# Attention in blocks of 32 keys, head pairs by quadrant, probabilities turned in place on VectorE

## The chip, the core and the metric

The kernel runs on one core of a Trainium2 chip. Its engines are named as in the profile: PE (TensorE, the 128x128 array for matrix products), PEld (its weight loads), DVE (VectorE), ACT (ScalarE), POOL (GpSimd) and SP (SyncE, which issues the transfers). The metric is the time of one execution in device microseconds; lower is better.

## What is computed

```python
# q, k, v: 8 batches x 8 heads x 576 x 64; x: 4608 x 512; w_in 512 x 1024, w_out 1024 x 512 (float64)
q_d, k_d, v_d = (means over 4 neighbours along the sequence)          # 144 rows each
out_up = repeat(softmax(scale * q_d @ k_d.T) @ v_d, 4)                # pooled attention
mask = abs(i - j) < 4
out_local = softmax(where(mask, scale * q @ k.T, -1e9)) @ v           # local attention
x = (out_up + out_local), heads side by side                          # 4608 x 512
h = x @ w_in
solu = h * softmax(h)
ln = (solu - mean) / sqrt(var + 1e-6) * g_ln
out = ln @ w_out                                                      # 4608 x 512
```

## The kernel before

The output rows fall into 36 FFN tiles of 128 rows. Each needs its rows of x, which attention makes batch by batch, 576 rows at a time, transposed: x lies with 128 partitions for the two heads of a pair and four pairs side by side.

**Local attention** of a batch is five units of two windows each, 64 keys for 58 queries. In a unit PE makes the scores (tile sc, L606 or L694: 16 fp32 matmuls, each on a 64x64 quarter of the array, which appear as 32 records in the trace), DVE adds the mask and takes the maximum, POOL or DVE subtracts it, ACT takes the exponential, DVE the sum and its reciprocal, POOL or DVE multiplies. The probabilities (pl) have to be turned. In batches 0 to 2 and in each batch's last unit PE does it (plt, L654, four transposes) and ACT or DVE copies the result out of PSUM (plT, L262 or L264). In batches 3 to 7 units go in pairs: eight transfers move 32-wide pieces (plT<-pl), and DVE transposes 128x1024 in 32x32 squares (L745). Then PE multiplies with the values (xp, L664 or L752), and the result is stored or added to x (L577).

**Pooled attention** goes by head pair, four times a batch: sd (L787, six matmuls of 144 keys), maximum (L794), three exponentials (L802), reciprocal and multiplication (L809, L811), 12 transposes on PE (pdt, L822), two copies (pdT), the product with the pooled values (po, L843), accumulation with each column written four times (L577).

**The FFN** splits x into a high and a low part in fp32r (xh, xl) and the weights likewise, and forms each product from three: h (L861, 24 matmuls of 128x512 for each half of 512 columns and both halves) and o (L985, 24). Between them stand the softmax chain (nmx, e, su, nmu), a trip through DRAM that turns u (u<-e, v<-u, then the DVE transposes of L962), and the split into uh and ul (L968, L971). The last tile's u is turned on PE (ut).

q and k of batches 0 and 1 are turned on PE (qp, kp, L556), later ones by DVE (L462, L466). The kernel also issues 24 pairs of filler matmuls (warm, L1042) in its first stages. PSUM: ps_a two buffers of two banks for everything of attention, ps_t one bank (plt, po), ps_h two banks (h), ps_o one bank (o).

All steps stand in a list, and the numbers in ORDER set the order in which they are issued; this is the order on every engine. A number that is also in OTHER swaps the engine of that step for its alternative (`engine(usual, instead)`). Nothing reorders at run time: an engine that waits holds up what stands behind it.

Of the kernel before, what the change touches and what calls it, by code (L numbers as in the profile page):

```python
# [136 lines left out]
def pooled_local_attention_then_solu_ffn(  # L137
# [33 lines left out]


# [980 lines left out]
```

## Time and profile before

| | us |
|---|---|
| median of 3 runs (lowest, highest) | 593.27 (591.71, 594.09) |
| span of the profiled execution | 592.8 |
| idle time of PE in the span | 24.3 |
| ACT busy, POOL busy | 335.9, 317.8 |
| moved by DMA | 99.58 MB in 207112 packets |

The page gives no time of the profiled execution other than its span, which is 0.5 us below the median. Busy times are sums over an engine's instructions. A PE matmul's start is recorded and its end modelled, so distances are taken from start to start. In a row of the trace, "sc<-kT,qT 64*64 64x64 f32 x32" means 32 records that make sc from kT and qT, with a tile of 64x64 of the array and 64 moving columns; the tiles that follow a "<-" with an engine in brackets are what the engine waited for. One fp32 matmul gives two records (two passes) and two weight loads.

### The profile page before, as it was taken

The page shows a single profiled execution, that of the slowest core. Times are in us where ns is not written, and L with a number is a line of the kernel's source. Part 1 is how long each engine was busy: PE and PEld are TensorE (multiplying, and loading weights), DVE is VectorE, ACT ScalarE, POOL GpSimd, SP SyncE. Part 2 cuts the span into 40 slices and gives each one's busy share as a digit, 9 for nine tenths or more (in the row PEclk, how much of TensorE's full clock was granted, in tenths as well). Part 3 has the DMA queues.
Part 4 walks back from the last instruction along what each step waited for, and adds up shares of the span by engine and source line. Part 5 has one row for each costly group of instructions (what it writes and reads, how often), then busy time and mean ns, then how long its engine had stood idle before and what let it go on. Part 6 is the DMA issues. An engine that isn't in the chain of part 4 may idle for free.

```text
span 592.8 us, 15179 instructions
## 1 busy us (share of the span) xinstructions
PE 568.5 (96%) x5832; PEld 439.3 (74%) x5832; DVE 468.1 (79%) x769; ACT 335.9 (57%) x751; POOL 317.8 (54%) x465
## 2 busy tenths in 40 slices
PE   8789799999989999999999999999999999999996
PEld 5567567677767777777777777787787777778885
DVE  6987999999898989887988968978885854654441
ACT  3577677785555655574457455575445645434443
POOL 2475799577765735485366734354532676242211
PEclk9698999999999999999999999999999999999999
DMA  9998779777787688785897858765535454332331
GB/s 272 237 239 168 162 178 201 184 143 210 178 190 179 147 235 183 173 209 169 194 187 186 203 155 156 214 150 177 159 101 159 133 143 139 106 126 90 124 108 53
DMA packets 207112, 99.58 MB, mean 168 GB/s; under 512 B 163136, under 2 KB 193344, under 8 KB 207040
## 3 DMA queue, kind: packets, MB, share of 16 engines
q1 hardware_dynamic: 207040, 98.61, 66.5%
q8 instruction: 46, 0.75, 0.6%
q14 instruction: 26, 0.21, 0.1%
HBM read 65.54 MB, written 27.79 MB: 157 GB/s over the span
## 4 chain that ended last, share of the span: by engine, by line
PE 72%; DVE 10%; SPq 4%; DMA 4%; issue 4%; POOL 3%; ACT 2%; DVEq 0%; POOLq 0%; ACTq 0%
PE h L861 28%; PE o L985 27%; SPq L285 3%; PE sd L787 2%; PE po L843 2%; PE xp L752 2%; PE pdt L822 2%; PE kp L556 2%; PE warm L1042 2%; PE qp L556 1%; PE sc L694 1%; DMA qm<-in_q_dram 1%; DMA u<-e 1%; POOL xl L1019 1%; PE sc L606 1%
## 5 line engine op out<-in xcount | busy, mean ns | idle before, releaser
L861 PE MATMUL h<-wi_h,xh 128*128 128x512 f32 x288 | 116.6, 405 | 0.9 <-DVE e L876 0.7
L985 PE MATMUL o<-wo_h,uh 128*128 128x512 f32 x288 | 116.4, 404 | 0.8 <-ACT uh L968 0.7
L861 PE MATMUL h<-wi_h,xl 128*128 128x512 f32 x288 | 114.3, 397 | 2.6 <-DVE xl L1019 1.4
L985 PE MATMUL o<-wo_l,uh 128*128 128x512 f32 x288 | 113.9, 395 | 0.0
L861 PE MATMUL h<-wi_l,xh 128*128 128x512 f32 x288 | 113.8, 395 | 0.0
L985 PE MATMUL o<-wo_h,ul 128*128 128x512 f32 x288 | 79.0, 395 | 0.0
L869 DVE TENSOR_REDUCE nmx<-h 128x1 f32<-128x1024 f32 x36 | 43.5, 1209 | 36.0 <-PE h L861 36.0
L873 ACT ACTIVATE e<-h,nmx 128x1024 f32<-128x1024 f32 x36 | 40.1, 1113 | 49.8 <-DVE nmx L869 46.0
L861 PEld LDWEIGHTS h<-wi_h,xl 128*128 128x128 f32 x288 | 54.1, 188 | 16.8 <-POOL xl L1019 2.0
L861 PEld LDWEIGHTS h<-wi_h,xh 128*128 128x128 f32 x288 | 54.1, 188 | 16.0 <-DVE e L876 1.9
L985 PEld LDWEIGHTS o<-wo_h,uh 128*128 128x128 f32 x288 | 54.0, 188 | 15.8 <-issue 1.6
L985 PEld LDWEIGHTS o<-wo_h,ul 128*128 128x128 f32 x288 | 54.0, 188 | 13.3 <-DVE ul L971 0.3
L861 PEld LDWEIGHTS h<-wi_l,xh 128*128 128x128 f32 x288 | 54.1, 188 | 12.0
L985 PEld LDWEIGHTS o<-wo_l,uh 128*128 128x128 f32 x288 | 54.1, 188 | 11.9
L971 POOL TENSOR_TENSOR ul<-v,uh 128x512 fp32r<-128x512 f32 x37 | 48.3, 1312 | 24.7 <-ACT uh L968 20.9
L876 DVE SCALAR_TENSOR_TENSOR e<-h,e 128x1024 f32<-128x1024 f32 x36 | 43.7, 1213 | 16.7 <-ACT e L873 16.5
L968 ACT ACTIVATE uh<-v 128x512 fp32r<-128x512 f32 x70 | 42.5, 623 | 21.0 <-DVE v L962 16.9
L962 DVE STREAM_TRANSPOSE v<-v 128x512 f32<-128x512 f32 x70 | 46.6, 688 | 4.8 <-DMA v<-u 4.8
L992 ACT ACTIVATE osb<-o,s 128x512 f32<-128x512 f32 x36 | 24.6, 682 | 43.3 <-PE o L985 18.3
L1019 POOL TENSOR_TENSOR xl<-x,xh 128x512 fp32r<-128x512 f32 (+1 forms) x31 | 37.6, 1219 | 16.5 <-ACT xh L1016 16.0
L881 POOL TENSOR_SCALAR nmu<-su 128x1 f32<-128x1 f32 x36 | 9.8, 273 | 67.0 <-DVE e L876 56.7
L899 ACT ACTIVATE e<-e,nmu 128x1024 f32<-128x1024 f32 x29 | 33.3, 1148 | 19.7 <-POOL nmu L881 19.7
(122 smaller groups left out, 1142.6 us busy)
## 6 DMA issues: line engine op xcount, KB each, us to landing
u<-e SPq DMA_DIRECT2D x35, 512.0 KB
v<-u SPq DMA_DIRECT2D x140, 128.0 KB
vs<-in_v_dram SPq DMA_DIRECT2D x32, 288.0 KB
out_dram<-osb SPq DMA_DIRECT2D x36, 256.0 KB
qm<-in_q_dram SPq DMA_DIRECT2D x96, 72.0 KB
km<-in_k_dram SPq DMA_DIRECT2D x96, 72.0 KB
vw<-in_v_dram SPq DMA_DIRECT2D x80, 64.0 KB
vw<-in_v_dram SPq DMA_DIRECT2D x40, 128.0 KB
```

The source lines that it names most:

```text
L285: nc.sync.dma_start(t[nm][Q * 32:Q * 32 + 32, pr], src[b, 2 * pr + par, :, dh * 32:dh * 32 + 32].rearrange("(k t) d -> t k d", t=32),)
L861: nc.tensor.matmul(hps[:, n, :], src[:, cc, :], wt[:, cc, n * 512:(n + 1) * 512], start=(cc == 0 and src is xh and wt is wi_h), stop=(cc = ...
L869: nc.vector.tensor_reduce(out=nmx, in_=hf, op=ALU.max, axis=AX.X, negate=True)
L873: nc.scalar.activation(e, hf, AF.Exp, bias=nmx, scale=1.0, accum_out=se)
L876: nc.vector.scalar_tensor_tensor(out=e, in0=hf, scalar=1.0, in1=e, op0=ALU.mult, op1=ALU.mult, accum_out=su)
L899: nc.scalar.activation(e, e, AF.Identity, bias=nmu, scale=1.0)
L962: nc.vector.transpose(vg, vg)
L968: nc.scalar.activation(uh, tp, AF.Copy)
L971: (usual if v is None else engine(usual, nc.vector)).tensor_tensor(out=ul, in0=tp, in1=uh.bitcast(F32), op=ALU.subtract)
L985: nc.tensor.matmul(o, src[:, j, :], wt[:, 4 * g + j, :], start=(g == 0 and j == 0 and src is uh and wt is wo_h), stop=(g == 1 and j == 3 a ...
L992: nc.scalar.activation(osb, o, AF.Copy, scale=s)
L1019: engine(nc.gpsimd, nc.vector).tensor_tensor(out=l, in0=src, in1=h.bitcast(F32), op=ALU.subtract)
```

## The change

- Windows of local attention have 32 keys for 24 queries. A unit holds eight windows (w selects one of four quadrants of 32 partitions, g one of two windows there), a batch three units. sc is 64 matmuls on 64x32 tiles of the array with 32 moving columns, twice as many tiles as before; xp comes in two halves of 32 matmuls on 32x64 tiles with 24 moving columns.
- Pooled attention goes by blocks of 29 queries, with the four head pairs in the four quadrants; five blocks in two slots, three and two. sd is 24 or 16 matmuls on 64x32 tiles; po two halves of 20 matmuls on 32x64 tiles with 87 or 58 moving columns.
- All keys of a window lie within one 32x32 square, so DVE turns the probabilities in place (in pl and pd), for every batch. The transposes on PE (plt, pdt), their copies, and the plT transfers are gone, and pl and pd are fixed buffers of three each.
- ps_t is gone; ps_o has two buffers; po uses ps_a.
- The values of a unit are loaded in four steps with two transfers each (64 KB, 32 rows x 8 heads x 64).
- ORDER and OTHER are new (places below). Paths that were switched off (MASKED, SUMS_ON_PE, G_LATE, FIRST_ON_PE) are removed. The FFN's code is the same.

The core of the diff:

```diff
-    W = 64
-    starts = [0] + [58 * w - 3 for w in range(1, 9)] + [S - W]
-    qlo = [58 * w for w in range(9)] + [520]
-    qhi = qlo[1:] + [S]
+    KB = 32
+    QW = 24
+    GW = 2
+    NU = S // (4 * GW * QW)
+
+    def window(u, w, g):
+        n = 4 * GW * u + GW * w + g
+        s0 = min(max(QW * n - (KB - QW) // 2 + 1, 0), S - KB)
+        return s0, QW * n - s0
+
+    QS = 29
+    SLOTS = ((0, 3), (3, 5))
+    QPAD = QS * 4 + KB
+    NKB = -(-SD // KB)
+    PDW = NKB * KB
...
-    ps_t = ctx.enter_context(tc.tile_pool(name="ps_t", bufs=1, space=PSUM))
     ps_h = ctx.enter_context(tc.tile_pool(name="ps_h", bufs=1, space=PSUM))
-    ps_o = ctx.enter_context(tc.tile_pool(name="ps_o", bufs=1, space=PSUM))
+    ps_o = ctx.enter_context(tc.tile_pool(name="ps_o", bufs=2, space=PSUM))
...
-    pls = [cpool.tile([P, NPR * LP], F32, name=f"pl_{n}") for n in range(4)]
+    NG = 2 * GW * NPR
+    pls = [cpool.tile([P, NG, KB + 1], F32, name=f"pl_{n}") for n in range(3)]
+    pds = [cpool.tile([P, 2, 3, PDW], F32, name=f"pd_{n}") for n in range(3)]
...
+    def load_vw(vw, b, u, w):
+        for g in range(GW):
+            s0, _ = window(u, w, g)
+            nc.sync.dma_start(
+                vw[w * KB:(w + 1) * KB, g], v[b, :, s0:s0 + KB, :].rearrange("h s d -> s h d")
+            )
...
+            sc = two_banks(*scores_bank(b, u), f"sc_{b}_{u}")[:, :, 0:GW * NPR * KB]
+            at = sc.rearrange("p a (g r k) -> p a g r k", g=GW, r=NPR)
+            for g in range(GW):
+                for pr in range(NPR):
+                    for n in range(8):
+                        w, par = n // 2, (n + n // 2) % 2
+                        s0, _ = window(u, w, g)
+                        nc.tensor.matmul(
+                            at[w * KB:(w + 1) * KB, par, g, pr],
+                            bt.qT[rows(par), pr, s0:s0 + KB], bt.kT[rows(par), pr, s0:s0 + KB],
+                            start=True, stop=True,
+                        )
+            yield
+            pl_all = pls[(NU * b + u) % len(pls)]
+            pl = pl_all[:, :, 0:KB]
+            mx = small.tile([P, NG], F32, tag="mxl", name=f"mxl_{b}_{u}")
...
+            engine(nc.gpsimd, nc.vector).tensor_tensor(
+                out=pl, in0=pl, in1=sm.unsqueeze(2).broadcast_to([P, NG, KB]), op=ALU.mult
+            )
+            yield
+            nc.vector.transpose(pl, pl)
+            yield
+            plT = pl.rearrange("p (a g r) k -> p a g r k", a=2, g=GW)
+            for half in range(2):
+                xp = two_banks(ps_a, "a", f"xp_{b}_{u}_{half}")[:, :, 0:NPR * GW * QW]
+                at = xp.rearrange("p a (r g n) -> p a r g n", r=NPR, g=GW)
+                for g in range(GW):
+                    for pr in range(NPR):
+                        for n in range(4):
+                            a, par = n // 2, (n + n // 2) % 2
+                            w = 2 * half + a
+                            _, a0 = window(u, w, g)
+                            ks = slice(w * KB, (w + 1) * KB)
+                            nc.tensor.matmul(
+                                at[rows(par), a, pr, g],
+                                bt.vw[u][ks, g, 2 * pr + par, :],
+                                plT[ks, par, g, pr, a0:a0 + QW], start=True, stop=True,
+                            )
                 yield
+                t0 = QW * GW * (4 * u + 2 * half)
+                accumulate(
+                    bt.out()[:, :, t0:t0 + 2 * GW * QW].rearrange("p r (a n) -> p r a n", a=2),
+                    xp.rearrange("p a (r n) -> p r a n", r=NPR), self.first,
...
+            sd = two_banks(*scores_bank(b, n), f"sd_{b}_{n}")[:, :, 0:ns * SD]
+            sd = sd.rearrange("p a (s k) -> p a s k", s=ns)
+            for s in range(ns):
+                for i in range(8):
+                    w, par = i // 2, (i + i // 2) % 2
+                    nc.tensor.matmul(
+                        sd[w * KB:(w + 1) * KB, par, s],
+                        qd_all[rows(par), w, QS * (s0 + s):QS * (s0 + s) + KB],
+                        bt.kd[rows(par), w, :], start=True, stop=True,
+                    )
...
+            pd_all = pds[(2 * b + n) % len(pds)][:, :, 0:ns]
+            pd = pd_all[:, :, :, 0:SD]
...
+            engine(nc.gpsimd, nc.vector).tensor_tensor(
+                out=pd, in0=pd, in1=sm.unsqueeze(3).broadcast_to([P, 2, ns, SD]), op=ALU.mult
+            )
+            yield
+            nc.vector.transpose(pd_all, pd_all)
+            yield
+            pdT = pd_all.rearrange("p a s (k q) -> p a s k q", k=NKB)
+            for half in range(2):
+                po = two_banks(ps_a, "a", f"po_{b}_{n}_{half}")[:, :, 0:ns * QS]
+                for kb in range(NKB):
+                    nk = min(KB, SD - kb * KB)
+                    for i in range(4):
+                        a, par = i // 2, (i + i // 2) % 2
+                        w = 2 * half + a
+                        ks = slice(w * KB, w * KB + nk)
+                        nc.tensor.matmul(
+                            po[rows(par), a].rearrange("p (s q) -> p s q", s=ns),
+                            bt.vd[ks, par, kb, :], pdT[ks, par, :, kb, 0:QS],
+                            start=kb == 0, stop=kb == NKB - 1,
+                        )
                 yield
+                q0 = QS * s0
+                xv = bt.out()[:, 2 * half:2 * half + 2, FAC * q0:FAC * (q0 + nq)]
+                accumulate(
+                    xv.rearrange("p r (s f) -> p r s f", f=FAC),
+                    po[:, :, 0:nq].unsqueeze(3).broadcast_to([P, 2, nq, FAC]), self.first,
                 )
                 yield
...
         late = bt.b == 0
+        local = [Local(bt, u, not late) for u in range(NU)]
+        pooled = [Pooled(bt, n, late) for n in range(2)]
+        values(bt)
         for it in pooled + local if late else local + pooled:
+            if isinstance(it, Local):
+                for w in range(4):
+                    step(bt.load_v, it.u, w)
+                row(it.steps(), 12)
+            else:
+                row(it.steps(), 10)
 
```

PE's order at one place in mid-run, before. Names are tile_batch_unit (sc, xp), tile_batch_pair (po) or tile_number (h, o); the last number of each is a running one. These rows stand between h_10 and the first half of o_7:

```order
L694 MATMUL sc_4_0_3346<-kT_4_2932,qT_4_3037 64x2x32 x16
L694 MATMUL sc_4_1_3364<-kT_4_2932,qT_4_3037 64x2x32 x16
L843 MATMUL po_3_1_3382<-pdT_3_1_3146,vd_3_3074 64x144 x4
L752 MATMUL xp_3_0_3387<-plT_3_0_3182,vw_3_0_2969 64x64 x16
L752 MATMUL xp_3_2_3404<-plT_3_2_2980,vw_3_2_3034 64x64 x16
L985 MATMUL o_7_3448<-wo_h_117,uh_7_0_3330 128x512
```

PE's order of the changed kernel ahead of the same o_7, which now comes behind h_9 (po_2_1_0 is batch 2, slot 1, half 0):

```order
L670 MATMUL h_9_3404<-wi_h_132,xl_9_3360 128x512
L531 MATMUL sc_3_2_3443<-kT_3_2800,qT_3_3053 32x32 x64
L531 MATMUL sc_3_0_3514<-kT_3_2800,qT_3_3053 32x32 x64
L531 MATMUL sc_3_1_3587<-kT_3_2800,qT_3_3053 32x32 x64
L647 MATMUL po_2_1_0_3684<-pd_2_122,vd_2_2194 64x58 x20
L794 MATMUL o_7_3731<-wo_h_134,uh_7_0_3509 128x512
```

The three sc of batch 3 have moved together; po stands behind them, and xp has moved elsewhere.

DVE's order, batch 3 in mid-run, before, at the turning of its pairs of units (mxd and rsd belong to pooled attention, v_7 to the FFN, qT_4 and kT_4 to the next batch):

```order
L264 COPY pdT_3_0_3165<-pdt_3_0_3152 72x6x48
L466 STREAM_TRANSPOSE qT_4_3037<-qm_4_2467 128x576
L264 COPY plT_3_4_3273<-plt_3_4_3167 128x512
L962 STREAM_TRANSPOSE v_7_3124<-v_7_3124 128x4x128 x2
L794 TENSOR_REDUCE mxd_3_2_3294<-sd_3_2_3246 128x3
L745 STREAM_TRANSPOSE plT_3_0_3182<-plT_3_0_3182 128x1024
L809 RECIPROCAL rsd_3_3_3323<-smd_3_3_3078 128x3
L745 STREAM_TRANSPOSE plT_3_2_2980<-plT_3_2_2980 128x1024
```

DVE's order of the changed kernel, from the sum of unit 0 of batch 3 to its turn:

```order
L555 TENSOR_REDUCE sml_3_0_3714<-pl_0_114 128x16
L556 RECIPROCAL sml_3_0_3714<-sml_3_0_3714 128x16
L780 TENSOR_TENSOR ul_7_1_3667<-v_7_3374,uh_7_1_3666 128x512
L771 STREAM_TRANSPOSE v_8_3657<-v_8_3657 128x4x128
L368 TENSOR_REDUCE qd_all_130<-qT_3_3053 128x144
L562 STREAM_TRANSPOSE pl_0_114<-pl_0_114 128x16x32
L414 STREAM_TRANSPOSE kT_4_3755<-km_4_3721 128x576
L233 COPY x_3_3842<-xp_3_0_0_3809 128x4x96
```

The turn (L562) has moved from a place long behind its unit's reciprocal to four rows behind it, and the copies of pdT and plT are gone; the values' product xp is stored two rows further on.

Of ORDER, 2039 numbers before and 1827 now, one line each:

```diff
-23 16 165 166 2 4 167 168 169 170 171 24 26 27 25 28 29 3 172 33 32 30 31 173 174 197 17 175
+1 32 22 9 24 147 148 26 27 34 35 149 131 25 28 150 33 151 152 132 133 134 29 153 135 136 137 30
```

More of the change, by code (lines that the diff above doesn't have):

```diff
@@ L271, in scores_bank @@
         return (ps_h, "h") if b < 1 and n % 2 else (ps_a, "a")
-    def small_bank(b, n):
-        return (ps_o, "o") if b < 2 and n % 2 and not WARM else (ps_t, "t")
     def load_q_k(t, b, pr):
@@ L434, in __getattr__ @@
             elif what == "qd":
-                self.qd = [
-                    qd_flat[:, (NPR - 1 - pr) * SD:(NPR - pr) * SD] for pr in range(NPR)
-                ]
+                self.qd = [qd_all[:, pr, 0:SD] for pr in range(NPR)]
             elif what == "kd":
@@ L475, in out, with pooled_vload, pooled_vsum @@
             return xs[self.b]
-        def value(self, kc, head):
-            return [self.vd[:, kc, head, :]]
-        def pooled_vload(self, c, hs):
-            self.vs[c, hs.start] = load_vs(self.b, c, hs)
-        def pooled_vsum(self, c, hs):
-            vs = self.vs.pop((c, hs.start))
+        def pooled_vload(self, n):
+            if n == 2:
+                self.vs[n] = tails[self.b % len(tails)]
+                load_tail(self.vs[n], self.b)
+                return
+            t = big(f"vs_{self.b}_{n}").rearrange("p (k x) -> p k x", k=NKB - 1)
+            load_vs(t, self.b, n)
+            self.vs[n] = t
+        def pooled_vsum(self, n):
+            vs = self.vs.pop(n)
+            out = self.vd[:, :, NKB - 1] if n == 2 else self.vd[:, n, 0:NKB - 1]
             eng = engine(nc.gpsimd, nc.vector)
@@ L489, in pooled_vsum @@
             eng.tensor_tensor(
[L490 removed]
+                out=out, in0=vs[:, :, 0:D], in1=vs[:, :, D:2 * D], op=ALU.add
             )
[L493 to L516 removed]
     class EarlyBatch(Batch):
@@ L593, in steps @@
             b = bt.b
-            early = b < MASKED
-            sc = two_banks(*scores_bank(b, u), f"sc_{b}_{u}")
-            if early:
-                for a in range(2):
-                    nc.tensor.matmul(
-                        sc[:, a, 0:NPR * W].rearrange("p (r w) -> p r w", w=W), ident_b,
-                        mask_b.unsqueeze(1).broadcast_to([P, NPR, W]), start=True, stop=False,
-                    )
-            for pr in range(NPR):
-                for par, wi in TILES:
-                    s0 = starts[2 * u + wi]
-                    nc.tensor.matmul(
-                        sc[rows(wi), par ^ wi, pr * W:(pr + 1) * W],
-                        bt.qT[rows(par), pr, s0:s0 + W], bt.kT[rows(par), pr, s0:s0 + W],
-                        start=not early, stop=not early or pr == NPR - 1,
-                    )
@@ L635, in steps @@
-            nc.scalar.activation(by_pair, by_pair, AF.Exp, scale=SCALE)
-            yield
-            sm = small.tile([P, NPR, 2], F32, tag="sml", name=f"sml_{b}_{u}")
-            nc.vector.tensor_reduce(
-                out=sm, in_=pl_all.rearrange("p (r a w) -> p r a w", r=NPR, a=2), op=ALU.add, axis=AX.X
-            )
-            rs = small.tile([P, NPR, 2], F32, tag="rsl", name=f"rsl_{b}_{u}")
-            nc.vector.reciprocal(out=rs, in_=sm)
+            sc = two_banks(*scores_bank(b, u), f"sc_{b}_{u}")[:, :, 0:GW * NPR * KB]
@@ L643, in steps @@
             yield
             engine(nc.gpsimd, nc.vector).tensor_tensor(
-                out=pl, in0=pl, in1=rs.unsqueeze(3).broadcast_to([P, NPR, 2, W]), op=ALU.mult
-            )
-            yield
-            q0, q1 = qlo[2 * u], qhi[2 * u + 1]
-            nw = (q1 - q0) // 2
-            a0 = [qlo[w] - starts[w] for w in (2 * u, 2 * u + 1)]
-            pool, tag = small_bank(b, u)
-            pt = pool.tile([P, NPR, 2, W], F32, tag=tag, name=f"plt_{b}_{u}")
-            for pr in range(NPR):
-                nc.tensor.transpose(pt[:, pr, :, :], by_pair[:, pr], ident)
@@ L655, in steps @@
-            yield
-            plT = wk.tile([P, NPR, 2, W], F32, tag="plT", name=f"plT_{b}_{u}")
-            copy(engine(nc.scalar, nc.vector), plT, pt)
-            yield
-            xp = two_banks(ps_a, "a", f"xp_{b}_{u}")
-            xp = xp[:, :, 0:NPR * W].rearrange("p a (r n) -> p a r n", r=NPR)[:, :, :, 0:nw]
-            for pr in range(NPR):
-                for row, par in TILES:
-                    wi = row ^ par
-                    nc.tensor.matmul(
-                        xp[rows(par), wi, pr, :], bt.vw[u][rows(row), wi, pr, :],
-                        plT[rows(row), pr, wi, a0[wi]:a0[wi] + nw], start=True, stop=True,
-                    )
@@ L720, in steps @@
+                out=pl, in0=pl, in1=mx.unsqueeze(2).broadcast_to([P, NG, KB]), op=ALU.subtract
             )
@@ L723, in steps @@
             yield
-            nc.vector.tensor_reduce(
-                out=mx, in_=by_head.rearrange("p c h k -> p h c k"), op=ALU.add, axis=AX.XY
-            )
-            nc.vector.tensor_scalar(out=mx, in0=mx, scalar1=1e-9, scalar2=None, op0=ALU.add)
-            nc.vector.reciprocal(out=mx, in_=mx)
+            sm = small.tile([P, NG], F32, tag="sml", name=f"sml_{b}_{u}")
+            nc.vector.tensor_reduce(out=sm, in_=pl_all, op=ALU.add, axis=AX.X)
+            nc.vector.reciprocal(out=sm, in_=sm)
@@ L745, in steps @@
-            nc.vector.transpose(plT, plT)
-            yield
-            plT = plT.rearrange("p (a n h q) -> p n h a q", a=2, n=2, q=32)
-            for n in range(2):
-                xp = two_banks(ps_a, "a", f"xp_{b}_{u + n}")
-                for pr in range(NPR):
-                    for wi, par in TILES:
-                        nc.tensor.matmul(
-                            xp[rows(par), wi, pr * W:(pr + 1) * W],
-                            bt.vw[u + n][rows(wi), 2 * pr + par, :],
-                            plT[rows(wi), n, par * NPR + pr], start=True, stop=True,
-                        )
-                yield
-                w0 = 2 * (u + n)
-                q0, q1 = qlo[w0], qhi[w0 + 1]
-                nw = (q1 - q0) // 2
-                a0, a1 = (qlo[w] - starts[w] for w in (w0, w0 + 1))
-                (p_step, _), (bank, _), _ = xp.ap
-                xp = bass.AP(
-                    tensor=xp.tensor, offset=xp.offset + a0,
-                    ap=[[p_step, P], [W, NPR], [bank + a1 - a0, 2], [1, nw]],
-                )
+            nc.vector.transpose(pl, pl)
@@ L806, in steps @@
+            pd = pd_all[:, :, :, 0:SD]
+            sm = small.tile([P, 2, ns], F32, tag="smd", name=f"smd_{b}_{n}")
+            for par in range(2):
+                for s in range(ns):
+                    nc.scalar.activation(
+                        pd[:, par, s], sd[:, par, s], AF.Exp, bias=mx[:, par, s:s + 1], scale=scale,
+                        accum_out=sm[:, par, s:s + 1],
+                    )
             nc.scalar.activation(sm, sm, AF.Copy, bias=FAC * 1e-9, scale=float(FAC))
             yield
-            rs = small.tile([P, QC], F32, tag="rsd", name=f"rsd_{b}_{pr}")
@@ L818, in steps @@
-            for kc in range(2):
-                for j in range(QC):
-                    for x in range(2):
-                        c = (2 * j + x) % QC
-                        nc.tensor.transpose(
-                            pt[:, x, kc, j, :], pd[rows(x), (0, 2, 1)[c], kc * 72:(kc + 1) * 72],
-                            ident[rows(x), rows(x)],
-                        )
-            pt = pt[:, :, :, :, 0:QN]
-            pdT = wk.tile([72, 2, QC, 2, QN], F32, tag="pdT", name=f"pdT_{b}_{pr}")
@@ L828, in steps @@
-            yield
-            copy(engine(nc.scalar, nc.vector), pdT[:, :, :, 0, :], pt[:, 0])
-            yield
-            copy(
-                engine(nc.scalar, nc.vector) if b < 2 else engine(nc.vector, nc.scalar),
-                pdT[:, :, :, 1, :], pt[:, 1],
-            )
-            yield
-            pdT = pdT.rearrange("p k j x n -> p k (j x n)")
-            pool, tag = small_bank(b, pr)
-            po = pool.tile([P, SD], F32, tag=tag, name=f"po_{b}_{pr}")
-            for kc in range(2):
-                for par in range(2):
-                    parts = bt.value(kc, 2 * pr + par)
-                    for n, vt in enumerate(parts):
-                        nc.tensor.matmul(
-                            po[par * 64:par * 64 + 64, :], vt, pdT[:, kc, par * SD:(par + 1) * SD],
-                            start=(kc == 0 and n == 0), stop=(kc == 1 and n == len(parts) - 1),
-                        )
```

279 lines of the change are left out of this document (48 added, 231 removed), and 190 rows, old and new, of tables (ORDER, OTHER).

## The prediction

> **What bounds the kernel now.** I read the page's totals first, then a table of busy time by stretch, then the engine timeline of PE inside one stretch, and last the DVE groups and the DMA queues. The totals, then six stretches (window, its length, busy us of PE, PEld, DVE, ACT and POOL, granted clock, DMA share, GB/s):
>
> ```profile
> span 592.8 us, 15179 instructions
> PE 568.5 (96%) x5832; PEld 439.3 (74%) x5832; DVE 468.1 (79%) x769; ACT 335.9 (57%) x751; POOL 317.8 (54%) x465
> ...
> 15.00:30.00 15.00, 10.59 (x126) 8.45 (x128) 14.17 (x23) 8.98 (x28) 6.54 (x6) 0.63 1.04 238
> 104.80:155.00 50.20, 48.86 (x536) 37.16 (x532) 46.20 (x81) 35.60 (x84) 34.59 (x48) 1.00 0.75 177
> 155.00:213.00 58.00, 55.51 (x556) 43.51 (x554) 53.94 (x86) 33.23 (x72) 37.42 (x54) 1.00 0.78 182
> 213.00:301.00 88.00, 88.00 (x1054) 69.11 (x1046) 74.46 (x119) 46.79 (x108) 45.92 (x68) 1.00 0.79 191
> 301.00:427.00 126.00, 126.00 (x1191) 98.72 (x1190) 107.05 (x173) 72.09 (x168) 66.56 (x105) 1.00 0.71 175
> 512.00:593.00 81.00, 75.94 (x337) 60.01 (x336) 37.48 (x59) 35.74 (x60) 21.52 (x57) 1.00 0.27 95
> ```
>
> PE is busy 96% of the span and without one gap from 213 to 427 us. There the time is what PE needs, and nothing else. Before 30 us DVE and the DMA engines (share 1.04) are full and PE waits; from 104.8 to 213 us PE loses 1.34 + 2.49 = 3.8 us while DVE stands at 92 to 93%. So two things count: PE's own work everywhere, DVE's work up to some 210 us.
>
> How PE's time divides is read from starts, because its ends are modelled. Pieces of PE's timeline (start, duration, group), from stretches where it does not idle:
>
> ```profile
> 110.67 0.53 PE L822 MATMUL pdt<-ident,pd 64*72 64x64 f32 x12
> 111.12 0.51 PE L861 MATMUL h<-wi_h,xh 128*128 128x512 f32 x1
> ...
> 120.84 0.71 PE L787 MATMUL sd<-kd,qd_flat 64*64 64x144 f32 x12
> 121.48 0.71 PE L843 MATMUL po<-pdT,vd 72*64 72x144 f32 x8
> 122.12 0.70 PE L606 MATMUL sc<-kT,qT 64*64 64x64 f32 x32
> 122.75 0.50 PE L985 MATMUL o<-wo_h,uh 128*128 128x512 f32 x1
> ...
> 153.32 0.66 PE L654 MATMUL plt<-ident,pl 128*128 128x128 f32 x4
> 153.91 1.16 PE L694 MATMUL sc<-kT,qT 64*64 64x64 f32 x64
> ...
> 215.20 0.40 PE L861 MATMUL h<-wi_h,xl 128*128 128x512 f32 x1
> 215.43 0.39 PE L861 MATMUL h<-wi_h,xh 128*128 128x512 f32 x1
> ...
> 218.70 0.40 PE L861 MATMUL h<-wi_h,xl 128*128 128x512 f32 x1
> 219.02 1.16 PE L694 MATMUL sc<-kT,qT 64*64 64x64 f32 x64
> 220.11 0.71 PE L843 MATMUL po<-pdT,vd 72*64 72x144 f32 x8
> 220.75 1.16 PE L752 MATMUL xp<-plT,vw 64*64 64x64 f32 x64
> 221.85 0.50 PE L985 MATMUL o<-wo_h,uh 128*128 128x512 f32 x1
> 222.18 0.40 PE L985 MATMUL o<-wo_l,uh 128*128 128x512 f32 x1
> ...
> 228.93 0.69 PE L694 MATMUL sc<-kT,qT 64*64 64x64 f32 x32
> 229.45 0.64 PE L664 MATMUL xp<-plT,vw 64*64 64x56 f32 x32
> 230.02 0.49 PE L861 MATMUL h<-wi_h,xh 128*128 128x512 f32 x1
> ```
>
> An FFN matmul starts about 0.233 us after the one before (15 starts from 215.20 to 218.70); 1728 of them take some 402 us, and the change leaves them alone. A run of 64 sc records takes 1.09 us, one of 32 takes 0.63: 32 more cost 0.46, so a record of a 64x64 tile costs 14.4 ns and a round over the four tiles 57.5. Each fp32 matmul is two records. What a run takes beyond that is overhead: 0.63 - 0.46 = 0.17 behind sc. A whole visit to attention pays about 0.36: 0.09 entering (218.70 to 219.02 less 0.233), 0.17 leaving, 0.10 more behind the first FFN matmul (221.85 to 222.18). Each change of tile shape inside a visit costs another 0.16 (sc to po: 1.09 less 64 x 14.4 ns).
>
> **The change on PE, step by step.** Durations are from the profiled execution, 592.8 us; the median, 593.27, is 0.5 above it.
>
> - sc: 40 units of 32 records at 14.4 ns are 18.4 us. Now 24 units of 128 records of 64x32 tiles, eight in use instead of four. The trace has no eight-tile run. If a tile again needs 57.5 ns for its step and eight run side by side, a record costs 7.2 ns and all 22.1 us; if PE cannot start records closer than 14.4 ns it is 44.2. I take 22.1, since the weights are half as wide, and keep 44.2 for the range. +3.7. [...]
> - xp: 18.4 us before. Now 48 halves of 64 records, again on four tiles at a time (K is 32, but the other half's row tiles stand idle), with 64 columns of weights and only 24 moving columns. Moving columns do not set this: 32 sc records and then 32 of xp with 56 columns took 1.09 us together (228.93 to 230.02), just as 64 with 64 columns did. So 3072 x 14.4 = 44.2, +25.8. If the shorter tile halved the step it would be 22.1.
> - sd: 12 records on four tiles, 0.64 less the 0.16 overhead, make four steps of 121 ns at 144 columns; 32 x 0.485 = 15.5 us. Now (3 + 2) x 2 steps of 121 ns per batch, eight tiles: 9.7. -5.8.
> - po: 15.5 by the same reckoning (8 records on two tiles). Now per batch 20 steps at 87 columns (121 x 87/144 = 73 ns) and 20 at 58 columns (the 57.5 floor): 2.61 x 8 = 20.9. +5.4.
> - TensorE transposes go: pdt 0.45 less 0.11 at its end, 32 times, -10.9; plt 0.59 less 0.16, 20 times, -8.6.
>
> That is +9.6 us of PE work, the reverse of what the word "smaller" suggests. Against it stands the new order. In the place shown of PE before o_7 a visit goes sc, sc, po, xp, xp with two changes of shape (64x64 tiles, po, 64x64 tiles) and two more visits follow within o_7; now the three sc of batch 3 stand together with one half of po, one change of shape in all. Counted over PE's whole order from h_3 on, visits fall from 48 to 36 and changes of shape inside them from 68 to 19. At 0.36 and 0.16 that is 28.2 before and 16.0 after: -12.2 us.
>
> Ahead of h_0 the order differs too: all three units of batch 0 are through before it, where two of five were, and more fillers stand between. That is work moved about before a start that DVE and the DMA engines set (15 to 30 us above), so I give it 0, with 5 us either way.
>
> **DVE, DMA and the other engines.** The groups (count, busy us, mean ns of one, idle before) and two queue lines:
>
> ```profile
> L962 DVE STREAM_TRANSPOSE v<-v 128x512 f32<-128x512 f32 x70 | 46.6, 688 | 4.8 <-DMA v<-u 4.8
> L971 DVE TENSOR_TENSOR ul<-v,uh 128x512 fp32r<-128x512 f32 x33 | 28.3, 864 | 5.1 <-ACT uh L968 4.2 <-POOL xl L1019 0.8
> L624 DVE TENSOR_TENSOR pl<-sc,mask 128x512 f32<-128x512 f32 x20 | 13.4, 675 | 1.5 <-PE sc L606 1.4
> L745 DVE STREAM_TRANSPOSE plT<-plT 128x1024 f32<-128x1024 f32 x10 | 12.2, 1225 | 3.3 <-DMA plT<-pl 3.3
> L710 DVE TENSOR_REDUCE mxl<-pl 128x16 f32<-128x1024 f32 x10 | 12.1, 1208 | 0.7 <-POOL pl L631 0.5
> L264 DVE COPY pdT<-pdt 72x288 f32<-72x288 f32 x21 | 8.9, 437 | 3.2 <-PE pdt L822 3.2
> L901 DVE TENSOR_SCALAR e<-e,nmu 128x1024 f32<-128x1024 f32 x6 | 5.1, 854 | 0.3 <-POOL nmu L881 0.3
> L644 POOL TENSOR_TENSOR pl<-pl,rsl 128x512 f32<-128x512 f32 x17 | 18.0, 1056 | 4.5 <-DVE rsl L642 4.5
> ...
> plT<-pl SPq DMA_DIRECT2D x80, 64.0 KB
> q8 instruction: 46, 0.75, 0.6%
> ```
>
> DVE: 40 mask adds become 24 (-10.8); maxima and sums of 20 x 512 and 10 x 1024 each become 24 x 512 each (-18.5); transposes were 10 x 1.225 and are 24 x 0.688 plus eight of 960 and eight of 640 columns (some 1.15 and 0.80): +19.9; copies of pdT go (-8.9); ul comes 10 times more to DVE (+8.6) and e - mean 12 times (+10.2); smaller counts (reciprocals, pooled maxima, value sums) give about -24. Net -23 of 468. This can return at most the 3.8 us PE lost between 104.8 and 213; I take 2.5, as part is for ACT and POOL. ACT and POOL lose work too and are under 60%. The 80 plT transfers go, and with them DVE's 3.3 us of waits on them; SP issues 192 value loads of 64 KB in place of 120, in stretches whose DMA share is 0.75 to 0.79, each meant for a unit well behind: 0.
>
> The turning in place adds a wait on DVE. Before, plT's transposes stood some forty rows behind their reciprocal and waited for a transfer; in the place shown of the changed kernel the turn stands four rows behind its reciprocal, and POOL's multiplication, 1.06 us, must fall between. Three DVE operations stand there (ul 0.86, v 0.69, qd some 0.7 us), so it costs 0. Without them kT, the x of xp and nmx of the next tile, all queued behind the turn, and PE's xp would wait up to 1.06 us, 24 times at worst. The second o bank lets a tile's o begin before the last is read out: no row of PE waits for that, 0.
>
> The end: PE's order now has all of h_35 ahead of o_33 and half of o_34 behind ut_35, so 2.8 us more work hides the last tile's chain and 2.8 us hide uh, for which o_35 waited 0.69 us:
>
> ```profile
> 582.99 0.50 PE L985 MATMUL o<-wo_h,uh 128*128 128x512 f32 x1 [0.69 <-ACT uh L968]
> ```
>
> I take -1.
>
> Sum: 592.8 + 9.6 - 12.2 - 2.5 - 1 = 586.7; the 30 us that PE loses in visits by a full count of starts, against my 28.2, takes another 0.7. Forecast 586.
>
> **Rivals.**
>
> PE's instruction supply (slower). 11664 PE records came in 46 packets: 254 to a packet. 0.6% of 16 engines over 592.8 us is 57 us, 1.24 us a packet. Now sc eats 256 records (128 weight loads, 128 matmuls) in 128 x 7.2 ns = 0.92 us, faster than one packet comes. Each of 24 units then loses 0.32 us at least, and up to 0.8, halfway to a whole packet's time (the whole is excluded: 46 packets at 1.24 us would have idled PE for 57 us before, and it idled 24): 8 to 20 us, 594 to 606, most likely 600. For it speaks a stop inside a run of sc that nothing released:
>
> ```profile
> 108.34 0.52 PE L606 MATMUL sc<-kT,qT 64*64 64x64 f32 x18
> 109.64 0.46 PE L606 MATMUL sc<-kT,qT 64*64 64x64 f32 x14 [0.78 <-issue]
> ```
>
> Against it: it is the only such stop, and the stretch from 213 to 301 us, with its 1054 matmul records, has none. It decides once fewer than two packets lie ready when three sc begin. Chance 0.16. [...]
>
> Eight tiles bring nothing: a floor lies under the spacing of records, whichever tile they go to, and 14.4 ns is it. sc then takes 44.2, +22, 608. For it: no row shows records closer on average. Against it: half the weight columns. Chance 0.12. [...]
>
> The new order brings waits: each of three probability buffers is held from its mask add to its second xp half, so a later mask add waits, PE stops at a full score bank, and half of the 14.7 us from visits and idle time is lost again. No change, 590 to 596. For it: DVE at 92% up to 213 us. Against it: DVE gets lighter. Chance 0.16.
>
> xp's step shortens with 32 rows: up to -22, so 564 to 578. [...] Chance 0.08.
>
> **How the numbers follow.** Forecast 586, chance 0.48, own range 580 to 590. Half a per cent, 3 us, is about what this kernel's measurement tells from no change. Faster: 0.48 + 0.08 = 0.56, of which the edge gives 0.01 to no change, so 0.55; slower: 0.12 and most of 0.16, 0.25; between: 0.20. The range leaves out the case of eight tiles (0.12) and the better part of the xp gain: 572 to 606.
>
> **What would show it.** sc of 128 records in about 0.92 us, 0.17 more at the end of a visit, and no packet's time between; xp halves of 64 in 0.93; sd of 24 matmuls in 0.73; 36 visits; PE without idle time from about 200 us; DVE near 445 us. The prediction is wrong if sc's runs stop on "issue", if a record of sc takes 14 ns, or if PE idles before xp or sc for pl or x.

## The result, and the profile after

The changed kernel takes 685.76 us (median of 4 runs, 684.60 to 686.62), the kernel before 592.90 (591.71 to 594.09). The ratio is 1.157, 95% interval 1.153 to 1.161: slower by a sixth, where 586 was forecast. From the page of the profiled execution: the totals of the span and of the engines, the granted clock in 40 slices, the queue that brings instructions, and the shares of the chain that ended last:

```profile
span 684.6 us, 23718 instructions
PE 611.6 (89%) x10232; PEld 487.7 (71%) x10232; DVE 442.3 (65%) x711; ACT 286.8 (42%) x619; POOL 253.4 (37%) x427
PEclk8955666699999989999899977998799979999999
q8 instruction: 80, 1.31, 0.8%
PE 85%; issue 8%; DMA 2%; ACT 2%; DVE 1%; SPq 1%; POOL 0%; ACTq 0%; DVEq 0%
```

PE now stands idle for 684.6 - 611.6 = 73.0 us; before it was 592.8 - 568.5 = 24.3. It has 2 x 10232 = 20464 records instead of 11664, and its instructions come in 80 packets instead of 46. What PE waited for (us in total, times, longest):

```profile
PE sc L531 <- issue: 28.4, 12, 3.6
PE po L647 <- issue: 7.4, 5, 2.6
PE sd L607 <- issue: 6.8, 3, 3.9
PE xp L575 <- issue: 6.1, 3, 4.1
```

"Issue" means that nothing the profile shows held PE back: no data, no bank, no semaphore. These four rows are 48.7 us. One such visit to attention, on the timeline of PE, and the FFN behind it:

```profile
320.26 2.17 PE L531 MATMUL sc<-kT,qT 64*32 64x32 f32 x230
324.66 1.31 PE L531 MATMUL sc<-kT,qT 64*32 64x32 f32 x128 [2.24 <-issue]
329.21 0.45 PE L531 MATMUL sc<-kT,qT 64*32 64x32 f32 x26 [3.25 <-issue]
329.59 0.79 PE L670 MATMUL h<-wi_h,xh 128*128 128x512 f32 x1
330.19 0.63 PE L670 MATMUL h<-wi_l,xh 128*128 128x512 f32 x1
330.61 0.63 PE L670 MATMUL h<-wi_h,xl 128*128 128x512 f32 x1
331.04 0.63 PE L670 MATMUL h<-wi_h,xh 128*128 128x512 f32 x1
```

The three units of sc, 384 records, stop twice. Between the stops PE runs exactly 128 matmuls, and 128 matmuls with their 128 weight loads are 256 instructions, one packet (20464 records in 80 packets are 256 to a packet). In the trace two packets of the instruction queue start in this stretch, at 322.37 and 326.75, 4.4 us apart. Behind it the FFN's matmuls start 0.42 to 0.43 us apart instead of the 0.233 of an undisturbed stretch: the granted clock from 329.6 to 333 us is 0.50. Both kernels by stage, cut at the start of h_0, the start of h_3 and the last tiles (window, length, busy us of PE, PEld, DVE, ACT, POOL, clock, DMA share, GB/s), before and then after:

```profile
0.00:65.40 65.40, 53.62 (x873) 38.97 (x873) 53.61 (x96) 40.05 (x98) 34.02 (x40) 0.87 0.93 222
65.40:104.80 39.40, 36.50 (x556) 26.39 (x552) 38.76 (x71) 29.15 (x69) 36.00 (x37) 1.00 0.85 184
104.80:583.00 478.20, 472.51 (x4389) 369.52 (x4385) 374.42 (x603) 264.41 (x581) 246.66 (x386) 1.00 0.63 161
```

```profile
0.00:92.20 92.20, 68.17 (x1693) 49.74 (x1693) 58.55 (x99) 35.29 (x74) 37.82 (x47) 0.70 0.74 175
92.20:149.70 57.50, 47.34 (x857) 37.76 (x854) 34.26 (x58) 27.52 (x63) 26.70 (x30) 0.74 0.58 129
149.70:675.00 525.30, 490.48 (x7666) 396.06 (x7666) 348.75 (x555) 221.09 (x477) 187.76 (x348) 0.94 0.56 138
```

The changed kernel loses 26.8 us before h_0, 18.1 from there to h_3 and 47.1 behind it. The clock's records in both traces hold 1.0 and 0.5 and nothing between, so 0.70 over 92.2 us is 55 us at half speed; the three stages of after make 55 + 30 + 63 = 148 us by these rounded figures, 147 by the records themselves. Before had 18, nearly all of it in the first stage. Reckoned over all of PE's starts, the 91.8 us between the spans are some 48 of idle time, some 20 by which FFN matmuls start further apart than 0.233, and some 20 more for attention's own records, some of it at half clock too; how the edges of a stop are counted shifts each of the three by 2 or 3 us.

### The profile page after: what moved, and what is told of

Its sections match the earlier page's. It is cut to its first block, busy times and chain, and to the rows that moved or that the text cites. A ratio compares the mean times of both kernels' runs of the same rounds, so it can differ in the third digit from the quotient of the medians.

```text
span 684.6 us, 23718 instructions
## 1 busy us (share of the span) xinstructions
PE 611.6 (89%) x10232; PEld 487.7 (71%) x10232; DVE 442.3 (65%) x711; ACT 286.8 (42%) x619; POOL 253.4 (37%) x427
## 4 chain that ended last, share of the span: by engine, by line
PE 85%; issue 8%; DMA 2%; ACT 2%; DVE 1%; SPq 1%; POOL 0%; ACTq 0%; DVEq 0%
PE h L670 32%; PE o L794 30%; PE xp L575 7%; PE po L647 5%; PE sc L531 4%; PE warm L851 2%; DMA km<-in_k_dram 2%; PE sd L607 2%; PE kp L487 2%; PE qp L487 1%; SPq L247 1%; ACT kT L231 0%; ACT x L231 0%; ACT pd L624 0%; DVE w L336 0%
## 5 line engine op out<-in xcount | busy, mean ns | idle before, releaser
L670 PE MATMUL h<-wi_h,xh 128*128 128x512 f32 x288 | 123.6, 429 | 1.4 <-DVE pl L562 1.4
L670 PE MATMUL h<-wi_l,xh 128*128 128x512 f32 x288 | 120.5, 418 | 1.1 <-issue 1.1
L670 PE MATMUL h<-wi_h,xl 128*128 128x512 f32 x288 | 119.9, 416 | 0.0
L670 PEld LDWEIGHTS h<-wi_h,xh 128*128 128x128 f32 x288 | 58.6, 203 | 16.0 <-issue 1.7
L670 PEld LDWEIGHTS h<-wi_h,xl 128*128 128x128 f32 x288 | 58.3, 202 | 15.9 <-POOL s L734 1.4
L670 PEld LDWEIGHTS h<-wi_l,xh 128*128 128x128 f32 x288 | 58.6, 203 | 14.7 <-issue 1.3
L575 PEld LDWEIGHTS xp<-pl,vw 32*64 32x64 f32 x3072 | 53.5, 146 | 21.9 <-issue 14.5
L575 PE MATMUL xp<-pl,vw 32*64 32x24 f32 x3072 | 57.6, 222 | 8.2 <-issue 6.1
L531 PE MATMUL sc<-kT,qT 64*32 64x32 f32 x3072 | 33.2, 210 | 31.2 <-issue 28.4
L531 PEld LDWEIGHTS sc<-kT,qT 64*32 64x32 f32 x3072 | 30.0, 112 | 34.9 <-issue 31.3
L771 DVE STREAM_TRANSPOSE v<-v 128x512 f32<-128x512 f32 x70 | 46.7, 690 | 10.6 <-DMA v<-u 10.3
```

The costliest lines, as they stand in the source:

```text
L531: nc.tensor.matmul(at[w * KB:(w + 1) * KB, par, g, pr], bt.qT[rows(par), pr, s0:s0 + KB], bt.kT[rows(par), pr, s0:s0 + KB], start=True, st ...
L575: nc.tensor.matmul(at[rows(par), a, pr, g], bt.vw[u][ks, g, 2 * pr + par, :], plT[ks, par, g, pr, a0:a0 + QW], start=True, stop=True,)
L670: nc.tensor.matmul(hps[:, n, :], src[:, cc, :], wt[:, cc, n * 512:(n + 1) * 512], start=(cc == 0 and src is xh and wt is wi_h), stop=(cc = ...
L771: nc.vector.transpose(vg, vg)
```

## The experiments

Two theories stood against each other at first. Supply (S): PE uses up instructions faster than packets come. Floor (F): small matmuls cannot start as close as the forecast had them, and "issue" is that. A third (W), waits of the new order for buffers and for DVE, is the milder rival.

**The kernel before, with its sc and xp matmuls cut in two.** The order, the units and the data stay; each matmul of 64 weight columns becomes two of 32, at four places like this (operands shortened):

```diff
-    nc.tensor.matmul(at[rows(wi), par, pr], qT[rows(par), pr, s0:s0 + W], kT[...])
+    for hh in range(2):
+        nc.tensor.matmul(at[wi * 64 + hh * 32:wi * 64 + hh * 32 + 32, par, pr],
+                         qT[rows(par), pr, s0 + hh * 32:s0 + hh * 32 + 32], kT[...])
```

> The kernel before, with each sc and xp matmul issued as two halves of the weight columns (64x32 tiles instead of 64x64): same products, same order, same data, 2560 more PE records, 16784 PE instructions instead of 11664. Theory S (PE's instructions come 256 at a time, about 4 us apart when PE has used up its store, and one packet lies ahead; what runs longer stalls, and the stall costs clock too): 8 to 15 us of new stalls that nothing releases, inside or behind runs of two sc or xp, some 3 us more for changes of shape, a few us at a lower granted clock: 602 to 620 us. [...] Theory W (the new order and the three probability buffers make PE wait): 593, as order and buffers are those of before.

It took 627.94 us (624.82 to 629.56), ratio 1.058 (1.051 to 1.064). The totals and the packets of its page, then three rows of PE's timeline, one with a stop in a run of xp and two without:

```profile
PE 593.1 (94%) x8392; PEld 457.8 (73%) x8392; DVE 469.6 (75%) x769; ACT 336.3 (54%) x751; POOL 314.7 (50%) x465
q8 instruction: 66, 1.08, 0.7%
...
242.35 0.71 PE L759 MATMUL xp<-plT,vw 64*32 64x64 f32 x47 [1.89 <-issue]
...
252.04 0.86 PE L699 MATMUL sc<-kT,qT 64*32 64x64 f32 x64
252.70 0.82 PE L667 MATMUL xp<-plT,vw 64*32 64x56 f32 x64
```

More instructions alone, in the old order with the old buffers, cost 35 us, so W cannot be the whole. PE's stops on issue come to 18.0 us, where before had 0.8. The supply theory's range is missed by 8 us. By starts, some 10 us of the 35 are more idle time, 7 slower FFN and 18 attention's own records, and most of the 18 is not a matter of supply: 64 records of a cut sc take 0.66 us (252.04 to 252.70), 10.3 ns each, where by the forecast's 7.2 two halves side by side would cost nothing. Over 5120 records the difference is 16 us. So by this reckoning about half of the 35 us is supply with its clock; the other half is that eight tiles do not halve the 14.4 ns.

**After, with fewer instructions.** In the first of two kernels a unit of sc is 16 matmuls on 64x64 tiles with 64 moving columns instead of 64 with 32, so that many scores belong to other keys; in the second xp is also cut from 32 matmuls a half to 16 with twice the columns, one window's values for both. Shapes of all other operations and the order stay (operands shortened):

```diff
-    for g in range(GW):
-        for pr in range(NPR):
-            for n in range(8):
-                nc.tensor.matmul(at[w * KB:(w + 1) * KB, par, g, pr], qT[..., s0:s0 + KB], kT[..., s0:s0 + KB])
+    for pr in range(NPR):
+        for n in range(4):
+            nc.tensor.matmul(at[w2 * 64:(w2 + 1) * 64, par, :, pr], qT[..., s0:s0 + 64], kT[..., s0:s0 + 64])
```

> The changed kernel with each unit's scores made by 16 matmuls on 64x64 tiles instead of 64 on 64x32 (the scores then belong to other keys; every later step runs on them as before): 4608 PE records... that is 2304 fewer matmul records and as many weight loads fewer, 15856 PE instructions instead of 20464, order and buffers unchanged. Theory S: stalls of PE fall from about 46 to about 5 us, PE work by 11, and most of the clock loss goes: 600 to 625 us. [...] Theory W: 670 to 680, the waits stay.

> As the run with a quarter of the sc matmuls, and each half of xp by 16 matmuls of 48 columns instead of 32 of 24 (one window's values for both): 12784 PE instructions, close to the 11664 of the kernel before. Theory S: no stall worth naming, granted clock back to about 0.98, 560 to 595 us, below the kernel before. [...] Theory W: 645 to 660.

With two runs each they took 608.27 us (606.63 to 609.91), ratio 1.026 (1.019 to 1.034), and 579.86 (577.82 to 581.89), ratio 0.978 (0.971 to 0.986). Against the kernel before that is too near 2% to tell; against the changed kernel's 685.76 it is 77 and 106 us less. PE's totals, packets and the largest stop on issue of the first:

```profile
PE 567.1 (94%) x7928; PEld 450.1 (74%) x7928; DVE 440.8 (73%) x711; ACT 286.6 (47%) x619; POOL 252.6 (42%) x427
q8 instruction: 62, 1.02, 0.7%
PE xp L574 <- issue: 4.7, 2, 3.8
```

Of the stops on issue in sc 0.2 us are left, and the second kernel has no stop on issue among PE's waits at all. In the first kernel h_3 starts at 127 us (before: 105, after: 150) and h_35 451 us later (before 460, after 507). Ahead of h_3 it still loses 22 us; behind h_3 it gains 9. It is not the forecast's kernel without the supply's limit, though: with 32 records a unit at 14.4 ns its sc costs 0.46 us a unit where the forecast had 0.92, and for the 18 units behind h_3 that alone is 8 us. The other terms of the forecast together bring about 1 us there.

**Streams on constants.** A kernel of its own, with no attention and no transfers: runs of 64x32-tile matmuls on eight tiles, 32 or 144 columns moving, between blocks of whole-array matmuls, and a last stream of whole-array matmuls of 64 columns (calls shortened to one line).

```diff
+    big("warm_a", 60); tiles("many32", 768, 32); big("warm_b", 60); tiles("many144", 768, 144)
+    big("warm_c", 60); tiles("run128", 64, 32);  big("warm_d", 60); tiles("run256", 128, 32)
+    big("warm_e", 60); tiles("run384", 192, 32); big("warm_f", 60); whole("whole128", 768, 128)
```

> Not the computation: streams of matmuls on constants, each behind 60 matmuls of 512 columns: 768 fp32 matmuls on 64x32 tiles with 32 columns (many32), the same with 144 columns (many144), runs of 64, 128 and 192 matmuls with 32 columns (run128, run256, run384, by records), then whole-array bf16 matmuls of 128 and of 64 columns, 768 each (whole128, whole64). Theory S: the first 256 to 512 instructions of many32 at 7 to 9 ns a record, then 128 records per 3.5 to 4.4 us, about 31 ns a record, with gaps; many144 ends at the same 31 ns although its tiles could do 15; run128 and run256 without a gap or with one, run384 with one or two; whole128 (128 matmuls in 7 us) without gaps; whole64 near the limit. [...]

Its PE timeline: the long streams of 32 and of 144 columns, the runs of 128 and 256 records, and the last stream. The second block is the two long streams (window, length, busy us of PE, PEld, DVE and POOL, granted clock, DMA share, GB/s):

```profile
17.51 1.57 PE L55 MATMUL many<-x 64*32 64x32 f32 x163
20.88 1.28 PE L55 MATMUL many<-x 64*32 64x32 f32 x128 [1.80 <-issue]
...
28.07 1.53 PE L55 MATMUL many<-x 64*32 64x32 f32 x128 [1.92 <-issue]
31.52 1.54 PE L55 MATMUL many<-x 64*32 64x32 f32 x128 [1.92 <-issue]
...
80.95 2.20 PE L55 MATMUL many<-x 64*32 64x144 f32 x128 [1.53 <-issue]
84.41 2.20 PE L55 MATMUL many<-x 64*32 64x144 f32 x128 [1.25 <-issue]
87.86 2.21 PE L55 MATMUL many<-x 64*32 64x144 f32 x128 [1.25 <-issue]
...
127.10 1.29 PE L55 MATMUL run<-x 64*32 64x32 f32 x128
128.32 13.12 PE L48 MATMUL warm_d<-wb 128*128 128x512 bf16 x58
141.37 2.21 PE L55 MATMUL run<-x 64*32 64x32 f32 x239
145.57 0.30 PE L55 MATMUL run<-x 64*32 64x32 f32 x17 [1.99 <-issue]
...
226.65 22.56 PE L64 MATMUL whole<-wb 128*128 128x64 bf16 x768 [0.28 <-DVE osb L43]
```

```profile
17.50:57.40 39.90, 17.83 (x1538) 16.50 (x1538) 0.19 (x1) 0.00 (x0) 0.58 0.02 5
72.50:114.00 41.50, 26.51 (x1537) 23.40 (x1536) 0.19 (x1) 0.00 (x0) 1.00 0.02 4
```

This decides between the two theories. A group of 256 instructions started mostly 3.45 us after the one before, now and then 3.73 and once 4.0, but in these streams never sooner, whether its work took 1.5 us or 2.2, with idle DMA engines around it (share 0.02). The last stream needed 256 instructions in 3.75 us (29 ns a matmul) and had no stop. A run of 128 records after a long block passed without a stop; the longer ones stopped after 163 to 239 records, 326 to 478 instructions, which is more than one packet and less than two. And the granted clock was 0.58 over the stream in which PE was busy 45% of the time, and 1.00 over the one in which it was busy 64%. The floor theory falls: 128 records passed in 1.22 us, 9.5 ns each with the change of shape in it.

**Fillers and the order.** If the clock before h_0 is what costs time there, more of the filler matmuls that keep PE busy should help; if long runs are what empties the supply, the same instructions further apart should.

```diff
 def keep_clock(n):
-    for _ in range(2):
+    for _ in range(8):
```

> The changed kernel with 8 filler matmuls (bf16, 512 columns) at each of the 24 filler places instead of 2, all of them ahead of h_2: 144 more of 0.22 us at full clock, 32 us of PE work. Theory S with clock (PE idles for want of instructions while the start runs, and falls to half clock for it): the fillers take the places of stalls and lift the duty, so the start is not longer by 32 but by at most 10 us, or shorter, and the granted clock ahead of h_0 goes from 0.70 to above 0.85: 675 to 696. If the start waits for something else than PE's instructions and clock (DMA, DVE), the same, as fillers fall into waits; if PE's work sets it at the clock given: 712 to 718.

It took 694.68 us (692.25 to 697.11, two runs), ratio 1.171 (1.165 to 1.177). 144 more fillers are 32 us of PE at full clock; the clock ahead of h_0 rose from 0.70 to 0.87 as forecast, h_0 came 15 us later and not at most 10, time at half clock fell from 147 to 111 us, and the end came 9 us later. Part of the fillers paid for itself; on the page's waits the stops of sc were no fewer:

```profile
PE sc L531 <- issue: 34.2, 14, 3.5
```

Two kernels moved many steps of attention on PE (sc, sd, po, xp), and what hangs on them, to places between FFN tiles: 52 steps in all, 20 of them on PE, and then 31 in all, with at least 16 us of PE work kept between a unit's sc and its xp. Only the table of the order differs.

> The changed kernel with the same steps and the same instructions on every engine; only the order differs: 20 steps of attention (sc, xp, sd, po) change places with neighbouring halves of FFN tiles, so that PE rarely meets more than 256 small-tile instructions without FFN matmuls between them. Theory S (PE is fed 256 instructions per 3.5 to 4.4 us, one packet ahead): of some 47 us of supply stalls some 28 go, and with them most spells at half clock after the first FFN tiles; the visits grow by about 10, 4 us: 630 to 655 us. Theory F (a floor under each small matmul): as many matmuls, no gain, 686 to 690. Theory W (waits for buffers and DVE): no gain or worse, 686 to 705, since each unit's chain starts later.

> As the first reordering, but 31 steps moved in place of 52, and none that leaves less than 16 us of PE work between a unit's sc and its xp (or sd and po, or h and o) where there was more. In the first one PE's stops for want of instructions had fallen from 53 to 34 us and h_15 came 13 us earlier, and from there on new waits for DVE and ACT (19 us) took it back; those waits should not come here. Theory S: stops for want of instructions 30 to 40 us, no new waits above 5 us, half-clock time below 120 us: 655 to 675 us. If the gain of order is always taken back, because DVE's and ACT's order was fitted to the stalls: 680 to 690. Theory F: 685 to 690 with no change in the stops.

Both missed: 688.41 us (686.17 to 691.69), ratio 1.161 (1.155 to 1.166), and 686.19 (682.02 to 688.83), ratio 1.157 (1.149 to 1.165). In the first, all its waits on issue fell from 52 to 39 us and h_15 started 13 us earlier than in after; in the second they fell to 40 and h_15 started 17 us earlier, though 7.5 of these were there at h_3, before any step had moved. New waits took it back (PE's waits of the first, then, from the timeline of the second, the chain of such a wait):

```profile
PE sc L531 <- issue: 17.4, 10, 2.9
PE xp L575 <- DVE pl L562: 6.9, 2, 6.0
PE po L647 <- DVE pd L636: 4.4, 1, 4.4
```

```profile
351.78 0.49 ACT L231 ACTIVATE x<-xp 128x384 f32<-128x384 f32 x1 [8.00 <-PE xp L575]
352.82 0.70 DVE L555 TENSOR_REDUCE sml<-pl 128x16 f32<-128x528 f32 x1 [7.27 <-ACT pl L552]
356.39 1.92 PE L575 MATMUL xp<-pl,vw 32*64 32x24 f32 x64 [4.67 <-DVE pl L562]
```

An xp moved later kept ACT 8.0 us at its store of x; the next unit's exponential stood behind that store on ACT, DVE's sum waited 7.3 us for it, and PE's next xp 4.7 us for the turned probabilities. So the last order moves little beside sc, whose results go to DVE: 6 of the 24 units are set apart from their neighbours, 14 steps in all. One place on PE:

```diff
 L647 MATMUL po_1_0_7942<-pd_121,vd_7295 64x58 x20
-L531 MATMUL sc_2_7964<-kT_7069,qT_7470 32x32 x64
-L531 MATMUL sc_1_8033<-kT_7069,qT_7470 32x32 x64
-L531 MATMUL sc_0_8106<-kT_7069,qT_7470 32x32 x64
-L647 MATMUL po_1_1_8173<-pd_121,vd_7295 64x58 x20
+L531 MATMUL sc_0_7971<-kT_7069,qT_7470 32x32 x64
+L647 MATMUL po_1_1_8038<-pd_121,vd_7295 64x58 x20
...
+L531 MATMUL sc_2_8076<-kT_7069,qT_7470 32x32 x64
 L670 MATMUL h_8143<-wi_h,xh_7830 128x512
...
+L531 MATMUL sc_1_8156<-kT_7069,qT_7470 32x32 x64
```

> Again only the order, and the least of it: six of the 24 sc (batches 2, 3, 4 and 7) are set apart from their neighbours by half an FFN tile, with the mask adds and what follows of three of them; no xp, sd or po moves. The second reordering was 17 us ahead of the changed kernel at h_15 and lost 16 of them between h_15 and h_18, where an xp moved late held up ACT's store of it and the exponential behind it. Theory S: that loss does not come here; some 16 us of stops for want of instructions go, and several spells at half clock: 655 to 672 us, with each gain to be seen at the batch where the sc stand apart (h_9, h_14, h_28) and kept. If the order is in balance with the stalls everywhere: 680 to 690.

It took 659.95 us (656.25 to 665.77), ratio 1.114 (1.105 to 1.124): 26 us less than after and inside the range put down for it, with the same instructions in the same 80 packets. PE's stops at sc, and one of the units that now stands alone, on the timeline:

```profile
PE sc L531 <- issue: 15.3, 8, 3.7
...
226.53 1.29 PE L531 MATMUL sc<-kT,qT 64*32 64x32 f32 x128
227.75 0.50 PE L670 MATMUL h<-wi_h,xh 128*128 128x512 f32 x1
```

The stops at sc fell by 13.1 us and the time at half clock from 147 to 104 us. Not all of this is the order: up to h_3 no step has moved, and yet h_3 starts at 140.3 us where it was 149.7 in after. In the second reordering, where nothing had moved up to there either, it started at 142.2; so the start differs by some 9 us between executions with the same order ahead of it, and what the order can claim are the 17 us behind h_3. There the stops at sc fell from 22.3 to 10.7 us and the time at half clock from 61 to 36. A unit alone went through in 1.22 us; in threes the second and third cost a stop of 1.8 to 3.6 us each.

## Why the prediction was wrong

**The step that failed is the price of a packet.** The rival of the instruction supply named the place, the sign and the row that spoke for it, and then priced it wrongly. It took the time that a packet's bytes are on their way, 1.24 us, as the interval between packets; the interval is 3.45 us in the stream and was 4.4 in the visit shown. So it put 8 to 20 us where PE's stops on issue came to 52. The trace of before held the interval already: around its only such stop, in sc at 108.34 to 109.64, two packets start at 106.99 and 111.06 us, 4.07 apart, and no two of its 46 are closer. In after's trace the closest two of the 80 start 3.31 us apart. And it excluded a whole packet's time since 46 of them would have idled PE for 57 us before. That does not follow: FFN matmuls use two instructions in 0.233 us, by which a packet of 256 lasts 30 us, and before had 0.8 us of stops on issue in all of its 46 packets; the stream's runs stopped only after 326 to 478 instructions. Behind h_3 a visit before held at most 136 small records, 272 instructions; now the longest four hold 424 to 464, and their sc alone is 768 instructions. With the right interval the size of the stops comes out. A packet of sc is used up in 1.22 us and the next one comes after 3.45 to 4.4, so each packet beyond those 326 to 478 instructions costs 2.2 to 3.2 us by this estimate; those four visits stop two or three times each, 4.9 to 7.3 us a visit and 23 in all, out of 33 us of stops on issue behind h_3. The other 19 lie ahead of it.

**The clock was not in the sum at all.** Stops of 2 to 4 us were followed by FFN at half clock (0.50, and 0.42 to 0.43 us between starts, behind the visit shown), some 20 us by starts. The two streams show both sides: with idle pieces of 1.9 us every 3.45 and PE busy 45% the clock was 0.58; with pieces of 1.25 and PE busy 64% it was 1.00. Whether the length of a piece or the share decides was not separated.

**The start, 0 with 5 either way, was +27, and +18 followed up to h_3.** The prediction said that DVE and the DMA engines set it. They did before (DMA share 0.93 up to h_0); in after DVE is busy 58.55 of 92.2 us where it had been 53.61 of 65.4. Twice as many records (1693 for 873) stand ahead of h_0, and PE has 19 us of stops on issue up to h_3 and a clock of 0.70 up to h_0. With fewer instructions the loss of 45 up to h_3 is 22 and 11 us in the two kernels, so about half of it or more goes with the number of instructions; some 9 us can be the start's own variation. How the rest divides between the clock, waits for the first transfers and more work ahead of h_0 was not separated.

**The terms that held.** From pieces of PE's timeline in after without a stop:

```profile
298.14 1.13 PE L575 MATMUL xp<-pl,vw 32*64 32x24 f32 x64
299.09 1.76 PE L647 MATMUL po<-pd,vd 32*64 32x87 f32 x80
300.79 0.50 PE L794 MATMUL o<-wo_h,uh 128*128 128x512 f32 x1
...
357.40 0.99 PE L607 MATMUL sd<-kd,qd_all 64*32 64x144 f32 x48
358.32 1.13 PE L575 MATMUL xp<-pl,vw 32*64 32x24 f32 x64
```

An xp half took 0.95 us for a forecast of 0.93: 64 records of 24 moving columns on four tiles at 14.8 ns each, where 64 columns had taken 14.4. sd of 24 matmuls took 0.92, less 0.16 for the change of shape 0.76, for 0.73. po of 80 records took 1.70, less 0.17 on leaving 1.53, for 1.46. sc was a little undersized: a unit alone takes 1.22 us where 0.92 + 0.17 was forecast, so 24 units cost 3 us more; the rival's floor of 14.4 ns a record was not there. (With 64 moving columns, in the kernel before cut in two, eight tiles gave 10.3 ns a record.) DVE has 442.3 us where 445 was forecast, but as PE now waits for instructions its relief returns nothing. The turn's wait was 0 but for one stop of 1.4 us at an FFN matmul. Behind h_3 the visits are 36, as counted, but that they and the shape changes return some 12 us is not shown: with a quarter of the sc matmuls, and 3 us of stops on issue left there, 9 us were gained, of which 8 are the smaller sc. What took the rest was not found. The second o bank was not tried by itself.

## What to carry to other kernels

Count TensorE's instructions as a resource with a rate: here 256 in 3.45 us in the stream, after 326 to 478 that passed without a stop, and an fp32 matmul counted for four (two records and two weight loads). Eight small tiles side by side took 9.5 ns a record here where four took 14.4, and the kernel had 20464 instructions on PE instead of 11664. A run of 128 such records passed without a stop and those of 256 and 384 did not. Two ways out were shown: long matmuls of the FFN between the runs (the last order took the stops at sc behind h_3 from 22.3 to 10.7 us) and larger tiles (0.2 us of stops at sc were left with a quarter of its matmuls). When a rate is read from a trace, take the interval between arrivals while the consumer starves, not the time that one arrival is in transit. And where a gain is credited to a new order, look first at the part of the run where the order is still the same.

## What was not expected of the hardware

- The refill of PE's instructions was one packet of 256 in 3.45 us, sometimes 3.73 or 4.0, in the two streams (DMA share 0.02), the same for packets of 1.5 and of 2.2 us of work; in the visit shown of after it was 4.4, and why was not separated.
- Eight tiles side by side passed 128 records of 32 moving columns in 1.22 us, 9.5 ns each with the change of shape in it; 64 records of 64 moving columns in 0.66, 10.3 ns each. Four tiles took 14.4 before, so twice the tiles did not halve it.
- The granted clock was 0.58 over the stream with PE 45% busy in pieces of 1.5 us, and 1.00 at 64% in pieces of 2.2; behind the two stops of the visit shown it was 0.50, and the FFN's matmuls started 0.42 to 0.43 us apart instead of 0.233.
- Taking a quarter of the stops away by another order (52 to 39 us on issue) brought nothing at all (688.41 us for 685.76): the time went into ACT's, DVE's and PE's waits for each other. Setting only the sc apart, whose results go to DVE, kept 17 us.
